# A spectral filter beside an expert router: the row transform split 64 by 32 instead of 128 by 16, in f32 on 64 by 64 pieces of the array

## The chip, the core and the metric

The kernel runs on one NeuronCore of a Trainium2 chip. The metric is device time in microseconds of one execution. The engines are named as in the profile: PE is TensorE's matmuls, PEld its weight loads, DVE VectorE, ACT ScalarE, POOL GpSimd, SP the engine whose queue issues the DMAs.

## What is computed

x is 2048 tokens by 576 numbers. After a layer norm two branches are added to x: A filters it in the two-dimensional Fourier domain, B is a router over 64 experts that picks, in each of 32 heads, the best of 8 keys twice.

```python
def _A_ref(x, w_r, w_i):
    X = rfft2(x, axes=(-2, -1))
    X = X * (w_r + 1j * w_i)
    return irfft2(X, (S, D), axes=(-2, -1))

def _B_ref(x, w_q, k1, k2, u, v):
    q = einsum("nd,dhc->nhc", xf, w_q)
    s1, s2 = q[..., :dk] @ k1.T, q[..., dk:] @ k2.T
    top_e = argmax(s1) * E + argmax(s2)
    act = gelu(einsum("nd,nhkd->nhk", xf, u[top_e]))
    return einsum("nhk,nhk,nhkd->nd", g, act, v[top_e])

xn = layernorm(x)
return x + _A_ref(xn, A_w_r, A_w_i) + _B_ref(xn, B_w_q, B_k1, B_k2, B_u, B_v)
```

With one expert for each head, g is 1. Since only the largest score matters, the kernel multiplies w_q by differences of keys (`fold_part`), and gets all scores of a token from x in one product (`scores`).

## The kernel before

The tokens are split 128 by 16: tile t holds the 128 tokens 16 n + t, so a transform over tokens is a transform of 128 points inside a tile and one of 16 points across tiles. In order of the data:

- `ln` takes the statistics of the tiles as they land (VectorE, for six tiles ACT). `folds(t)` folds the 576 columns twice, about 288 and about 144, into cosine and sine parts (names `t` and `A` in the profile), scales the 128-point matrix by the tile's deviation (`Rs`) and copies the 33 leftover columns three times (`yl`).
- `dft128(t)` multiplies in f32: four matmuls `Rs,A` and two `Rs,yl`. An f32 matmul leaves two records in the trace, one for each pass. The product is parted into f16 high and low halves in `AB` (ACT, then VectorE), the leftover columns in `ABL`, whose rows 0 to 32, 33 to 65 and 66 to 98 hold the low and twice the high half.
- `fold_part(b, s)` is the product with the keys, f32, four pieces of 32 columns side by side (`w,KP`), on data that arrive by 32 transfers of 576 KB through five buffers; `fold_scale`, `fold_end` and `fold_last` bring it to `MU` and `MUL` in f16 halves.
- `d_fwd(g)` does the column transform for one sixteenth of the frequencies, out of `AB` and `ABL` (needs all sixteen `dft128`); its result is again parted in f16 halves (`A`). `s_fwd(g)` does the 16-point transform of two groups, 48 f16 matmuls on four 64 by 64 pieces of the array. `s_mul(g)` multiplies by the filter: two products on VectorE (`t`), two sums on GpSimd (`y`), a parting into f16 halves (`yh`) on ACT and GpSimd, and the leftover columns (`yl`) on ACT.
- `s_inv(g)` transforms back, 36 f16 matmuls on two 64-row pieces; `AB` and `ABL` are written again.
- `scores(r)`, `route(r)` and `combine(r)` treat two tiles of tokens each: 28 matmuls of 512 columns, the maxima and masks on VectorE, and the gathered weights `CAT` (inside `MT`).
- `d_inv(t)` is the column transform back (evicted by ACT, VectorE and GpSimd), `fin(t)` the 128-point transform back (f32, `A,c`) with the experts' sum (`vS,MT`) in the same PSUM tile; VectorE adds x and SP writes out.

`allmax` gets scales for the f16 halves as largest values: a transpose on TensorE, a maximum on VectorE, a matmul that spreads it.

The order of all instructions is made while the program is built: `_Plan` records operations, and `forward` places them by a table of priorities (`RANK`), its own costs, and PSUM places with limits for each kind of tile. All are issued through one helper line, so every row of the profile has the line L527 and is told apart by its tiles.

Of the kernel before, what the change touches and what calls it, by code (L numbers as in the profile page):

```python
# [10 lines left out]
F32 = mybir.dt.float32  # L11
# [4 lines left out]
OP = mybir.AluOpType  # L16
AX = mybir.AxisListType.X
# [14 lines left out]

def _consts():
    pi2 = 2 * np.pi
    n1 = np.arange(128)
    R = np.zeros((128, 16, 4, 2))
    for k in range(64):
        g, a = divmod(k, 4)
        if k == 0:
            R[:, g, a, 0] = 1.0  # L40
            R[:, g, a, 1] = (-1.0) ** n1
        else:
            R[:, g, a, 0] = np.cos(pi2 * (k * n1 % 128) / 128)
            R[:, g, a, 1] = -np.sin(pi2 * (k * n1 % 128) / 128)
    R = _clean(R.reshape(128, 128))
    c32 = np.stack([R * 2.0 ** -7, R.T * 0.5, np.eye(128)], 1).astype(np.float32)

    U = np.zeros((16, 16, 4, 2, 16, 2, 4))
    V = np.zeros_like(U)
    n2 = np.arange(16)[:, None]  # L50
    k2 = np.arange(16)[None, :]
    kk = np.zeros((16, 16, 2, 4), int)
    for g in range(16):
        for a in range(4):
            k1 = 4 * g + a
            if k1 == 0:
                for s in range(2):
                    ph = pi2 * ((64 * s + 128 * k2) * n2 % 2048) / 2048
                    U[g, :, a, s, :, s, a] = np.cos(ph)
                    V[g, :, a, s, :, s, a] = -np.sin(ph)  # L60
                    kk[g, :, s, a] = 64 * s + 128 * np.arange(16)
            else:
                ph = pi2 * ((k1 + 128 * k2) * n2 % 2048) / 2048
                for s, sg in ((0, 1), (1, -1)):
                    U[g, :, a, 0, :, s, a] = np.cos(ph)
                    U[g, :, a, 1, :, s, a] = np.sin(ph)
                    V[g, :, a, 0, :, s, a] = -sg * np.sin(ph)
                    V[g, :, a, 1, :, s, a] = sg * np.cos(ph)
                    kk[g, :, s, a] = (sg * (k1 + 128 * np.arange(16))) % 2048
    U = _clean(U.reshape(16, 128, 128))  # L70
    V = _clean(V.reshape(16, 128, 128))
# [7 lines left out]
    def halves(m):  # L79
        return np.concatenate([m[:, :64, :64], m[:, 64:, 64:]], 1)  # L80
# [50 lines left out]
    return c32, c16, s16, kk, ll  # L131


INF = float("inf")

CHANGE = 97.0

# [159 lines left out]
class _Plan:  # L297
# [7 lines left out]
    def cost(self, eng, m, out, ins, kw):  # L305
        n = 1
# [927 lines left out]
```

## Time and profile before

| | |
|---|---|
| median of 3 runs | 222.79 us (221.79 to 223.17) |
| span of the profiled execution | 220.8 us (its own time is not given apart) |
| moved by DMA | 43.43 MB, 197 GB/s in the mean |
| largest loads | wq: 32 of 576 KB; xT: 16 of 320 KB; W: 8 of 578 KB; x: 3 of 1154 KB and 2 of 577 KB |

The page cuts the span into 40 slices of 5.5 us; each digit is the busy share of a slice in tenths, PEclk the clock granted to TensorE:

```profile
PE   0079789999999999899998999899999899999993
DVE  1886999998599879639999998999999999999973
ACT  2096987986499788986769658585652323332330
POOL 3987887960209962854598349687946656686890
PEclk9999999999999999999999999999999999999999
DMA  6999999999999991634246310410000012123225
```

TensorE begins at the third slice. The DMA engines are full in the first fifteen slices and have little to do after that. From the twentieth slice TensorE and VectorE are both near full, while ACT empties towards the end.

### The profile page before, as it was taken

How to read it: one execution, taken by the hardware profiler on the slowest of the kernel's cores; microseconds unless marked ns; L12 is line 12 of the kernel's file. 1: busy time of each engine (PE TensorE's matmuls, PEld its weight loads, DVE VectorE, ACT ScalarE, POOL GpSimd, SP SyncE). 2: the span in 40 equal slices, each digit the busy share in tenths (PEclk: the TensorE clock that was granted, in tenths of full speed). 3: DMA queues.
4: the chain of work that ended last, by engine and by line, in shares of the span. 5: the costliest groups of instructions: out<-in, count | busy, mean ns of one | idle time of the engine just before them, and what ended most of it. 6: DMA issues, size and time to landing. Idle time of an engine off the chain costs nothing.

```text
span 220.8 us, 5961 instructions
## 1 busy us (share of the span) xinstructions
PE 196.7 (89%) x2287; PEld 134.9 (61%) x2287; DVE 193.2 (88%) x423; ACT 136.8 (62%) x297; POOL 146.0 (66%) x201
## 2 busy tenths in 40 slices
PE   0079789999999999899998999899999899999993
PEld 0048367766866658466565666455566577788872
DVE  1886999998599879639999998999999999999973
ACT  2096987986499788986769658585652323332330
POOL 3987887960209962854598349687946656686890
PEclk9999999999999999999999999999999999999999
DMA  6999999999999991634246310410000012123225
GB/s 205 405 425 416 408 410 405 389 354 353 367 410 411 406 370 64 202 98 109 96 123 196 118 56 11 148 39 4 1 3 0 0 56 107 53 109 125 91 113 210
DMA packets 14572, 43.43 MB, mean 197 GB/s; under 512 B 1872, under 2 KB 4688, under 8 KB 14160
## 3 DMA queue, kind: packets, MB, share of 16 engines
q1 hardware_dynamic: 14544, 43.05, 52.5%
q8 instruction: 18, 0.29, 0.5%
q14 instruction: 10, 0.08, 0.1%
HBM read 38.33 MB, written 4.72 MB: 195 GB/s over the span
## 4 chain that ended last, share of the span: by engine, by line
PE 48%; DVE 23%; ACT 13%; issue 6%; DMA 5%; POOL 3%; SPq 0%; DVEq 0%; POOLq 0%; ACTq 0%
PE banks L527 48%; DVE t L527 5%; DMA xf<-in_xT_dram 4%; DVE w L527 4%; DVE MT L527 3%; DVE A L527 3%; ACT t L527 2%; ACT xf L527 2%; DVE mx L527 2%; DVE AB L527 2%; DMA kT<-in_kT_dram 2%; ACT AB L527 1%; POOL yh L527 1%; DVE st L527 1%; ACT A L527 1%
## 5 line engine op out<-in xcount | busy, mean ns | idle before, releaser
L527 PE MATMUL banks<-MU,xT 128*128 128x512 f16 x192 | 47.9, 379 | 1.0 <-ACT A L527 0.6
L527 POOL TENSOR_TENSOR xT<-xf,xT 128x640 f16<-128x640 f32 x16 | 23.2, 1455 | 19.5 <-ACT xf L527 19.5
L527 PE MATMUL banks<-c,AB 128*128 128x145 f16 (+1 forms) x384 | 34.6, 227 | 0.0
L527 PEld LDWEIGHTS <-xT 128*128 128x128 f16 x224 | 20.6, 99 | 21.9 <-issue 1.3
L527 PEld LDWEIGHTS <-AB 128*128 128x128 f16 x384 | 31.7, 122 | 3.4 <-issue 1.6
L527 POOL TENSOR_TENSOR A<-t 128x145 f32<-128x145 f32 (+2 forms) x48 | 30.3, 647 | 4.0 <-DVE t L527 1.5
L527 POOL TENSOR_TENSOR y<-t,t 128x289 f32<-128x289 f32 x32 | 21.6, 697 | 14.7 <-DVE t L527 14.5
L527 POOL TENSOR_TENSOR yh<-y,yh 128x578 f16<-128x578 f32 x16 | 23.4, 1470 | 6.8 <-issue 3.0
L527 POOL TENSOR_TENSOR t<-XN 128x289 f32<-128x289 f32 x32 | 24.9, 799 | 4.3 <-DVE A L527 3.0
L527 DVE SCALAR_TENSOR_TENSOR t<-banks,wx,Wt 128x578 f32<-128x578 f32 x32 | 24.3, 808 | 0.3 <-PE banks L527 0.3
L527 DVE TENSOR_TENSOR AB<-banks,AB 128x512 f16<-128x512 f32 x32 | 21.6, 679 | 1.9 <-ACT AB L527 1.1
L527 PE MATMUL banks<-w,KP 128*32 128x288 f32 x256 | 21.5, 432 | 1.8 <-DMA w<-in_wq_dram 1.5
L527 ACT ACTIVATE yh<-banks,sc 128x580 f32<-128x580 f32 x16 | 11.7, 744 | 17.6 <-PE banks L527 13.6
L527 PE MATMUL banks<-Rs,yl 128*99 128x128 f32 x64 | 10.9, 302 | 13.1 <-ACT Rs L527 13.1
L527 ACT ACTIVATE AB<-banks 128x512 f16<-128x512 f32 x32 | 18.8, 590 | 4.6 <-PE banks L527 4.5
L527 PE MATMUL banks<-A,c 128*128 128x288 f32 x64 | 21.4, 416 | 0.0
L527 PE MATMUL banks<-c,ABL 99*128 99x289 f16 (+1 forms) x64 | 18.5, 289 | 2.3 <-DVE AB L527 0.9
L527 PEld LDWEIGHTS banks<-Rs,A 128*128 128x128 f32 x128 | 16.3, 202 | 3.7 <-DVE A L527 1.8
L527 DVE TENSOR_TENSOR ABL<-banks,ABL 33x256 f16<-33x256 f32 x32 | 12.9, 407 | 6.4 <-ACT AB L527 5.3
L527 PEld LDWEIGHTS banks<-Rs,yl 128*99 128x99 f32 x64 | 8.3, 180 | 16.6 <-ACT Rs L527 15.7
L527 PE MATMUL banks<-Rs,A 128*128 128x128 f32 x128 | 18.2, 292 | 0.0
L527 DVE TENSOR_REDUCE MT<-w 128x128 bf16<-128x896 bf16 (+1 forms) x16 | 18.1, 1143 | 0.1
(124 smaller groups left out, 433.5 us busy)
## 6 DMA issues: line engine op xcount, KB each, us to landing
w<-in_wq_dram SPq DMA_DIRECT2D x32, 576.0 KB, 7.6
xf<-in_xT_dram SPq DMA_DIRECT2D x16, 320.0 KB, 4.6
Wt<-in_W_dram SPq DMA_DIRECT2D x8, 578.0 KB, 7.3
out_dram<-XN SPq DMA_DIRECT2D x14, 288.0 KB, 2.1
XN<-in_x_dram SPq DMA_DIRECT2D x3, 1154.0 KB, 12.4
s<-in_s_dram SPq DMA_DIRECT2D x16, 192.0 KB, 3.4
XN<-in_x_dram SPq DMA_DIRECT2D x2, 577.0 KB, 4.9
c<-in_c_dram SPq DMA_DIRECT2D x1, 868.5 KB, 8.6
```

What stands on the lines that cost most here:

```text
L527: fn(*[x.place() if isinstance(x, _Ps) else x for x in args], **{k: x.place() if isinstance(x, _Ps) else x for k, x in kw.items()})
```

## The change

The tokens are split 64 by 32. A tile now holds two sets of 64 tokens, one in each half of the partitions, and the host puts rows and columns of x, W, v and the result into the order that this needs (`_tokens`, `_columns`). What follows from it, and what else is done:

- `folds` folds once; the second fold is done by `dft128`, which adds two f32 matmuls into one PSUM place, on two 64-row pieces. VectorE makes one sum of 289 numbers; GpSimd makes one difference, and copies the leftover columns for 14 tiles; seven scalings move from ACT to VectorE. Two more tiles have their statistics on ACT.
- `d_fwd`, `s_fwd`, `s_mul` and `s_inv` keep f32: no f16 halves of `A` and `y` are made. `s_fwd` is 16 f32 matmuls and `s_inv` 16, both on four 64 by 64 pieces. The leftover columns of two groups are transformed by `s_left`, parted, and stacked in `ABL` by six transfers (42 in all); the last two groups have `s_last`, without transfers.
- The second product of the filter for groups 4 to 15 is a copy on ACT and a product on GpSimd.
- `scores` has 24 and 2 matmuls, and four on 64 by 64 pieces. The maximum over seven keys is three pairwise steps. Four `xT` halves are parted on VectorE.
- `d_inv` takes `ABL` last; the second half of the even-odd sum is on GpSimd for six tiles and on VectorE for ten. `fin` takes two tiles: 8 f32 matmuls on 64 by 64 pieces, 4 on 64-row pieces and 4 whole ones.
- Scales come from `root`, a sum of squares by one matmul and a root by arithmetic on the float's bits, in ten places; one `allmax` is left.
- Sixteen matmuls on a constant tile stand first on TensorE.
- The order and the PSUM places are now lists of numbers (`ORDER`, `BANK`), and each GpSimd instruction with inputs waits for the last VectorE instruction ahead of it in the list that is marked as using their shared port.

The core of the diff:

```diff
+                if o.port and o.eng == "gpsimd" and held is not None:
+                    tc.add_manual_dep(o.last.ins, held.last.ins.name, WAIT, reason="the shared port")
+            if o.port and o.eng == "vector":
+                held = o
...
+    wu = AB[:, 0, 0, 0:512]
+    V.memset(wu, 1.0)
+    pw_ = PS("m", (128, 512))
+    for k in range(16):
+        P.matmul(pw_, wu[:, 0:128], wu, start=True, stop=True)
...
+    def root(src, k, dst, e):
+        p = PS("m", (128, 64))
+        P.matmul(p[:, :k], on[:, 0:1].to_broadcast([128, 128]), src, start=True, stop=True)
...
+        V.tensor_scalar(dst.bitcast(I32), v, 0.5, float(0x1FBD1DF5 + (e << 23)), op0=OP.mult, op1=OP.add)
...
     def folds(t):
-        G.tensor_tensor(F[:, 1, 0:145], e[:, 1, 0:145], e[:, 1, 288:143:-1], op=OP.add)
-        V.scalar_tensor_tensor(F[:, 0, 0:145], e[:, 0, 0:145], rr[:, 2, t:t + 1], e[:, 0, 288:143:-1],
-                               op0=OP.add, op1=OP.add)
-        (V if t in DV else G).tensor_tensor(F[:, :, 145:289], e[:, :, 143::-1], e[:, :, 145:289], op=OP.subtract)
...
+        e = T([128, 2, L], F32, "e", 4, "A2")
+        G.tensor_tensor(e[:, 1], xn[:, 0:L], xn[:, L:], op=OP.subtract)
...
+            V.scalar_tensor_tensor(e[:, 0], xn[:, 0:L], rr[:, 2, t:t + 1], xn[:, L:], op0=OP.add, op1=OP.add)
+        Rs = T([128, 2, 64], F32, "Rs", 3)
+        if t in RV:
+            V.tensor_scalar(Rs, Rm, rr[:, 0, t:t + 1], None, op0=OP.mult)
+        else:
+            A.activation(Rs, Rm, AF.Copy, scale=rr[:, 0, t:t + 1])
+        fl = T([128, 2, 3, 33], F32, "fl", 4, "y")
+        if t in FG:
+            G.tensor_copy(fl, e[:, :, 0:33].unsqueeze(2).to_broadcast([128, 2, 3, 33]))
+        else:
+            A.activation(fl, e[:, :, 0:33].unsqueeze(2).to_broadcast([128, 2, 3, 33]), AF.Copy)
...
-        for c in range(4):
-            b, s = divmod(c, 2)
-            o = 161 if s else 0
-            P.matmul(p[:, 0, 128 * c:128 * c + 128], F[:, b, o:o + 128], Rs, start=True, stop=True)
...
+        sm = [Rs[r, 0:1].to_broadcast([64, 2, 64]) for r in hs]
         for b in range(2):
-            P.matmul(p[:99, 1, 128 * b:128 * b + 128], FL[:, b, :, :].rearrange("p a b -> p (a b)"), Rs, start=True, stop=True)
+            for h, r in enumerate(hs):
+                P.matmul(p[:, h, 128 * b:128 * b + 128], e[r, b, 34:289:2], sm[h], start=True, stop=False, tile_position=(64 * h, 0))
...
+            for h, r in enumerate(hs):
+                P.matmul(p[:, h, 128 * b:128 * b + 128], e[r, b, 33:288:2], Rs[r], start=False,
+                         stop=True, tile_position=(64 * h, 0))
+        for b in range(2):
+            for h, r in enumerate(hs):
+                P.matmul(p[:99, h, 256 + 64 * b:320 + 64 * b], fl[r, b], Rs[r, 0], start=True,
+                         stop=True, tile_position=(64 * h, 0))
...
-        allmax(wm[:, g // 2:(g + n) // 2], n // 2, wx[:, 0, g:g + n].rearrange("p (k e) -> p k e", e=2), 4096.0)
+        root(wm[:, g // 2:(g + n) // 2], n // 2, wx[:, 0, g:g + n].rearrange("p (k e) -> p k e", e=2), 13)
...
-        t = T([128, 2, 2, L], F16, "A2", 2)
-        A.activation(t[:, 0], p[:, :, :L], AF.Copy)
-        V.tensor_tensor(t[:, 1], p[:, :, :L], t[:, 0], op=OP.subtract)
+        t = T([128, 2, L], F32, "A2", 4)
+        A.activation(t, p[:, :, :L], AF.Copy)
...
-                for ha, hb in ((0, 0), (1, 0), (0, 1)):
...
-                            s = S16[g + q][:, :384].rearrange("p (h w) -> p h w", h=2)
-                            P.matmul(ps[q][o:o + 64, m, :L], s[r, ha, 64 * w:64 * w + 64], A2[g + q][r, hb, b, :],
-                                     start=(n == 0), stop=(n == 5), tile_position=(64 * e, o))
-                    n += 1
+                for e in range(2):
+                    r = slice(64 * e, 64 * e + 64)
+                    for q in range(2):
+                        o = 64 * (e ^ q)
+                        P.matmul(ps[q][o:o + 64, m, :L], S32[g + q][r, 64 * w:64 * w + 64], A2[g + q][r, b, :],
+                                 start=(b == 0), stop=(b == 1), tile_position=(64 * e, o))
...
+        if g in SG:
+            A.activation(t2, p[:, :, :L], AF.Copy, scale=sw)
+            G.tensor_tensor(t2, t2, wi, op=OP.mult)
+        else:
+            V.scalar_tensor_tensor(t2, p[:, :, :L], sw, wi, op0=OP.mult, op1=OP.mult)
...
-        yh = T([128, 2, 2, L], F16, "yh", 2)
-        A.activation(yh[:, 0], y, AF.Copy)
-        G.tensor_tensor(yh[:, 1], y, yh[:, 0], op=OP.subtract)
...
-        Y[g] = (yh, yl)
+        Y[g] = y
...
-        for c in range(3):
+        y, s = Y[g], S32[g][:, 192:]
+        for c in range(2):
             for ri in range(2):
+                for z in range(2):
                     for e in range(2):
+                        r, o = slice(64 * e, 64 * e + 64), 64 * (e ^ z)
+                        P.matmul(p[o:o + 64, e ^ g % 2, c, :], y[r, ri, 161 * c + o:161 * c + o + 64],
+                                 s[r, 64 * ri:64 * ri + 128], start=(ri == 0), stop=(ri == 1), tile_position=(64 * e, o))
...
+    def s_left(g):
+        p = PS("c")
+        for ri in range(2):
+            for q in range(2):
+                y, s = Y[g + q], S32[g + q][:, 192:]
+                for e in range(2):
+                    r, o = slice(64 * e, 64 * e + 64), 64 * (e ^ q)
+                    P.matmul(p[o:o + 64, q, :128], y[r, ri, 128:192], s[r, 64 * ri:64 * ri + 128], start=(ri == 0),
+                             stop=(ri == 1), tile_position=(64 * e, o))
...
+        for k, n in ((1, 0), (2, 0), (0, 1)):
+            for e in range(2):
+                to = ABL[33 * k:33 * k + 33].rearrange("p b (a e n) -> p (b a) e n", a=2, e=2)
+                Q.dma_start(to[:, :, e, 32 * g:32 * g + 64], h[64 * e:64 * e + 33, n])
...
-            P.matmul(p[:, b, :290], ABLt[:99, b, :, t], il[:99, b, :], start=True, stop=False)
...
+        plan.cut()
+        for b in range(2):
+            P.matmul(p[:, b, :290], ABLt[:99, b, :, t], il[:99, b, :], start=False, stop=True)
...
+    EG = (0, 3, 6, 8, 11, 14)
...
-    def fin(t, y):
-            hs = slice(288 * h, 288 * h + 288)
-            P.matmul(p[:, h, :288], RT, y[:, hs], start=True, stop=False)
-            for q in range(2):
-                P.matmul(p[:, h, :288], CAT[:, t, :], vS[:, q, hs], start=False, stop=(q == 1))
...
+    def fin(t, ys):
...
+            for z in range(2):
+                for i in range(2):
+                    o = 64 * (z ^ i)
+                    P.matmul(ps[i][o:o + 64, h, :L], RT[64 * z:64 * z + 64], ys[i][64 * z:64 * z + 64, h],
+                             start=True, stop=False, tile_position=(64 * z, o))
+        for h in range(2):
+            for i in range(2):
+                r = slice(64 * i, 64 * i + 64)
+                P.matmul(ps[i][:, h, :L], CAT[r, t + i, :], vS[r, 1, L * h:L * h + L], start=False, stop=False,
+                         tile_position=(64 * i, 0))
+        plan.pack = set()
+        for i in range(2):
+            for h in range(2):
+                P.matmul(ps[i][:, h, :L], CAT[:, t + i, :], vS[:, 0, L * h:L * h + L], start=False, stop=True)
```

Where the lists move work, three places. On TensorE at the start of the program before (`yl` and `A` are the leftover columns and the folded tile, `w` a part of wq; x2 and x4 count matmuls in a row):

```order
L527 MATMUL banks<-Rs_102,yl_104 99x128 x2
L527 MATMUL banks<-Rs_103,yl_105 99x128 x2
L527 MATMUL banks<-w_119,KP 32x288 x4
L527 MATMUL banks<-w_118,KP 32x288 x4
L527 MATMUL banks<-Rs_103,A_1_99 128x128 x4
L527 MATMUL banks<-Rs_102,A_0_98 128x128 x4
```

and now, from the last of the sixteen constant matmuls on (`U` holds the leftover columns):

```order
L321 MATMUL banks<-AB 128x512
L321 MATMUL banks<-Rs_101,A_0_97 128x128 x8
L321 MATMUL banks<-Rs_101,U 99x64 x4
L321 MATMUL banks<-Rs_101,A_3_100 128x128 x8
L321 MATMUL banks<-Rs_101,U 99x64 x4
L321 MATMUL banks<-Rs_103,A_2_99 128x128 x8
```

The first pieces of wq have moved behind seven tiles of `dft128`.

On TensorE in the last stage before, one tile's `d_inv` ends and `fin` follows (`c` beside `AB` is the column matrix, beside `A` the matrix of `fin`):

```order
L527 MATMUL banks<-c_72,AB 128x145
L527 MATMUL banks<-A_0_98,c_68 128x288
L527 LDWEIGHTS MT
L527 MATMUL banks<-vS,MT 128x288
L527 LDWEIGHTS MT
L527 MATMUL banks<-vS,MT 128x288
```

and now, where the first pair's `fin` follows the `d_inv` of tile 4:

```order
L321 MATMUL banks<-c_72,ABL 128x290
L321 MATMUL banks<-A_0_97,c_68 64x289
L321 MATMUL banks<-A_1_98,c_68 64x289
L321 MATMUL banks<-A_0_97,c_68 64x289
L321 MATMUL banks<-A_1_98,c_68 64x289
```

The pieces of the two tiles alternate, and `ABL` has moved behind `AB`.

On SP's queue now, behind the last transfer of wq (`lo` are the parted leftover columns, `xf` the loads of xT, `Wt` the filter):

```order
L321 DMA ABL<-lo_131 33x4x64 x2
L321 DMA xf_122<-in_xT_dram 128x640
L321 DMA ABL<-lo_130 33x4x64
L321 DMA mk<-in_mk_dram 128x99
L321 DMA Wt_109<-in_W_dram 128x1156
L321 DMA ABL<-lo_130 33x4x64
L321 DMA xf_123<-in_xT_dram 128x640
```

Loads of xT and of the filter now stand behind transfers that wait for ACT and VectorE.

More of the change, by code (lines that the diff above doesn't have):

```diff
@@ L252 @@
 class _Op:
[L253 to L273 removed]
+    __slots__ = ("tiles", "eng", "calls", "cols", "stage", "port", "last")
 def size_of(dt):
@@ L643, in g @@
             plan.stage += 1
+            plan.names[plan.stage] = (f.__name__, *(x for x in args if isinstance(x, int)))
             return f(*args)
@@ L1124, in _body @@
+    for t, n in ((0, 1), (1, 3), (4, 4), (8, 4), (12, 4)):
         ln(t, n)
@@ L1169, in _body @@
         s_inv(g)
+        if g > 13:
+            s_last(g)
+        elif g % 2:
+            s_left(g - 1)
         if g + 2 < 16:
```

715 lines of the change are left out of this document (275 added, 440 removed), and 128 rows, old and new, of tables (BANK, ORDER, RANK).

## The prediction

> **What bounds the kernel now.** I read the page's head and chain first, then the busy times by stage, then TensorE's timeline for the price of each piece of work, then VectorE's groups. Head and chain of the page:
>
> ```profile
> span 220.8 us, 5961 instructions
> PE 196.7 (89%) x2287; PEld 134.9 (61%) x2287; DVE 193.2 (88%) x423; ACT 136.8 (62%) x297; POOL 146.0 (66%) x201
> PE 48%; DVE 23%; ACT 13%; issue 6%; DMA 5%; POOL 3%; SPq 0%; DVEq 0%; POOLq 0%; ACTq 0%
> ```
>
> Two engines are nearly full, so a change must relieve both. The kernel has one sharp seam: `d_fwd` needs all sixteen `dft128`, and the first matmul behind the last of them (uv_prep's `Wt,on`) starts at 54.95. The windows view split there (columns: length, then busy time of each engine, granted clock, DMA share, GB/s):
>
> ```profile
> core 0: us, PE busy (x) PEld busy (x) DVE busy (x) ACT busy (x) POOL busy (x), PEclk, DMA share, GB/s
> 0.00:54.95 54.95, 39.86 (x350) 28.03 (x350) 45.28 (x138) 38.03 (x106) 38.78 (x73) 1.00 0.98 377
> 54.95:217.40 162.45, 156.86 (x1941) 106.92 (x1937) 147.44 (x285) 98.78 (x192) 107.19 (x128) 1.00 0.38 137
> ```
>
> Stage 1, up to the seam, belongs to VectorE (45.28 us, while PE also has to wait for it); stage 2 belongs to TensorE (156.86 of 162.45) with VectorE 9% behind. Then 3.4 us follow. I forecast the three lengths apart.
>
> TensorE's prices come from its timeline, as start to next start where nothing waited (columns: start, length, instruction, count; an f32 matmul leaves two records, one for each pass, and the pairs of rows are not all adjacent):
>
> ```profile
> 42.55 0.60 PE L527 MATMUL banks<-Rs,yl 128*99 128x128 f32 x4
> 42.99 1.06 PE L527 MATMUL banks<-Rs,A 128*128 128x128 f32 x8
> 43.88 0.60 PE L527 MATMUL banks<-Rs,yl 128*99 128x128 f32 x4
> ...
> 49.19 0.69 PE L527 MATMUL banks<-w,KP 128*32 128x288 f32 x8
> 49.81 1.16 PE L527 MATMUL banks<-Rs,A 128*128 128x128 f32 x8
> ...
> 53.85 1.18 PE L527 MATMUL banks<-w,KP 128*32 128x288 f32 x16
> 54.95 1.10 PE L527 MATMUL banks<-Wt,on 128*128 128x64 f32 x8
> ...
> 110.02 1.68 PE L527 MATMUL banks<-A,s 64*64 64x289 f16 x48
> 111.63 1.04 PE L527 MATMUL banks<-MU,xT 128*128 128x512 f16 x4
> ...
> 120.11 0.84 PE L527 MATMUL banks<-s,yh 64*128 64x128 f16 x24
> 120.79 0.50 PE L527 MATMUL banks<-s,yl 64*99 64x128 f16 x12
> 121.22 1.04 PE L527 MATMUL banks<-MU,xT 128*128 128x512 f16 x4
> ...
> 142.47 2.76 PE L527 MATMUL banks<-MU,xT 128*128 128x512 f16 x12
> 145.07 0.27 PE L527 MATMUL banks<-c,wm 128*1 128x128 f32 x1
> ...
> 199.32 0.65 PE L527 MATMUL banks<-A,c 128*128 128x288 f32 x2
> 199.81 0.41 PE L527 MATMUL banks<-vS,MT 128*128 128x288 f16 x2
> 200.05 0.65 PE L527 MATMUL banks<-A,c 128*128 128x288 f32 x2
> ...
> 216.89 0.29 PE L527 MATMUL banks<-vS,MT 128*128 128x288 f16 x1
> ```
>
> So: an f32 pass over 128 columns costs 0.89/8 = 0.111 us, over 288 columns 0.49/2 = 0.245 (199.32 to 199.81). Four f32 pieces side by side, 32 columns of the array each, take 0.49 for eight passes (1.10 for 16 less 0.62 for 8): 0.061 a pass, exactly a quarter of 0.245. A pair in `s_fwd` is 1.61 for 48 f16 pieces of 64 by 64; one `s_inv` 0.68 + 0.43 = 1.11; 512 f16 columns 2.60/12 = 0.217; an f16 288-column matmul 0.12; a half tile of `fin` 0.73.
>
> **The change, part by part.** The VectorE groups that it touches (columns behind the bar: busy us, mean ns of one), and one GpSimd group:
>
> ```profile
> L527 DVE TENSOR_TENSOR A<-t 128x288 f32<-128x288 f32 x16 | 8.1, 504 | 1.9 <-PE banks L527 1.4 <-POOL t L527 0.6
> L527 DVE SCALAR_TENSOR_TENSOR A<-t,rr 128x145 f32<-128x145 f32 x16 | 6.5, 414 | 0.0
> L527 DVE BATCH_NORM_STATS2 st<-XN 128x6 f32<-128x288 f32 x20 | 7.8, 444 | 3.7 <-DMA XN<-in_x_dram 3.7
> L527 DVE CAST wt<-mk 128x448 bf16<-128x448 f32 x1 | 1.0, 1003 | 0.0
> L527 DVE TENSOR_TENSOR A<-banks,A 128x578 f16<-128x578 f32 x16 | 11.9, 751 | 0.5 <-ACT A L527 0.4
> L527 DVE SCALAR_TENSOR_TENSOR t<-banks,wx,Wt 128x578 f32<-128x578 f32 x32 | 24.3, 808 | 0.3 <-PE banks L527 0.3
> L527 DVE SCALAR_TENSOR_TENSOR t<-banks,sc,yh 128x290 f32<-128x290 f32 x16 | 8.2, 512 | 0.7 <-ACT yh L527 0.6
> L527 POOL TENSOR_TENSOR yh<-y,yh 128x578 f16<-128x578 f32 x16 | 23.4, 1470 | 6.8 <-issue 3.0 <-ACT yh L527 2.2 <-POOL y L527 1.5
> ```
>
> Stage 1 goes by VectorE. From its 45.28 us fall 16 second folds (8.1), 16 short sums (6.5), four statistics (1.8; the mean is 0.444) and the cast that now stands behind the seam (1.0). In come 16 sums of 289 numbers, not shown before: 0.414 is the price of half the width, 0.512 that of 290 from PSUM; I take 0.5, nearest to the second, 8.0 in all. In come 7 scalings of 128 numbers: between 0 and 0.414, taken as 0.2, so 1.4. Left are 37.3. VectorE's first work came at 4.63, and idled 54.95 - 4.63 - 45.28 = 5.0 inside the stage:
>
> ```profile
> 4.63 1.54 DVE L527 BATCH_NORM_STATS2 st<-XN 128x6 f32<-128x288 f32 x4 [3.66 <-DMA XN<-in_x_dram]
> ...
> 10.80 0.85 DVE L527 SCALAR_TENSOR_TENSOR A<-t,rr 128x145 f32<-128x145 f32 x1
> ```
>
> The first load is one tile in place of two, so I start at 3.9 and keep 2 of the 5 idle: the seam lies at 3.9 + 37.3 + 2 = 43.2. Lowest: no idle, scalings free, sums at 0.414: 38.4. Highest: all 5 idle, scalings at 0.414, sums at 0.85 as in the last row, which has half the width: 53.3. ACT's 38.0 loses 14 copies and 7 scalings and gains the sums of two tiles and three squarings: even, and next in line behind VectorE. GpSimd's 38.8 falls by a second fold and an addition a tile. TensorE is no limit there: a tile of `dft128` was 0.44 + 0.89 = 1.33, and is now 16 passes two side by side (0.89) and 8 short ones, between 0.22 (64 columns at a quarter of 0.111) and 0.48 (0.119 a pass in the `Wt,on` row, half of it): at most 1.37. The 16 dummy matmuls stand ahead of all data; their cover is the wait for x.
>
> Stage 2 goes by TensorE, against 162.45:
> - fold matmuls: 52 stood behind the seam, now 80: 56 passes at 0.061, +3.4.
> - `s_fwd`: 48 f16 pieces become 16 f32 pieces, 32 passes of 289 columns, a quarter of 0.245 each: 1.96 for 1.51 without the shape switch, eight pairs: +3.6.
> - `s_inv`: 1.11 becomes 32 passes at a quarter of 0.111, 0.89; `s_left` adds 16 such passes in 7 pairs, `s_last` two times 16: 14.2 + 3.1 + 0.9 for 17.8, +0.4.
> - `scores`: two of 28 matmuls of 0.217 become four pieces side by side (0.22): -0.2 each of eight, -1.7.
> - `fin`: a pair of tiles was 4 x 0.73 = 2.93; now 16 passes at 0.061, four half-height pieces two by two (0.24) and four whole ones (0.49): 1.71. Eight pairs: -9.9.
> - ten guards lose one of two short matmuls, about 0.11 from start to start (145.07 stands for it): -1.1.
> - switches between piece shapes: 63 behind the seam in both orders, 0.
>
> Sum -5.3. VectorE there loses the 16 low halves (12.0) and twelve products (9.7), gains ten second halves in `d_inv` (5.1 at 0.512), so its 147.4 falls to about 131, 83% of the stage, and should not hold TensorE. The twelve products go to ACT (12 copies) and GpSimd (12 at 1.47, while 16 subtractions of the same size leave it). I keep the stage's other 5.6 us (162.45 - 156.86) as they are: 157.15. The 42 row transfers of `s_left` stand ahead of loads on SP's queue:
>
> ```profile
> L527 SPq DMA_DIRECT2D w<-in_wq_dram x32: 327/328/647, 3.5 to 72.7; - x32
> out_dram<-XN SPq DMA_DIRECT2D x4, 144.0 KB, 1.8
> ```
>
> At 0.33 us an issue they take 13.8 us of a queue that is nearly idle, and land in 1.8 us or more (the smallest transfer shown). The cover is `scores(7)` and four `s_inv` between the last of them and `d_inv(0)`, some 10 us; without it the first `d_inv` would stand 2 to 4 us. The new waits of GpSimd for VectorE cost GpSimd up to one VectorE instruction each; behind them stand the y sums that `s_inv` needs, and GpSimd's idle third covers it. What they save VectorE I leave out.
>
> The end was 220.8 - 217.4 = 3.4; three of four halves now pass VectorE after nearly the same matmul, one more of about half a microsecond: 4.0.
>
> **Sum.** 43.2 + 157.15 + 4.0 = 204.35 us of span, for 220.8. The median of the runs, 222.79, lies 1.99 over this span (no separate time of the profiled execution is given), so 206.3.
>
> **Rivals.** *Slower: the f32 pieces run two at a time.* In `s_fwd`, `fin` and `s_left` the two row halves write one PSUM bank at once. Were they to take turns, 256 + 128 passes would cost 0.061 more and 112 passes 0.028 more: +26.6, 233. It decides from 62% of that on. Against it: the row at 110.02 has the same arrangement in f16, 48 pieces in 1.61, 0.034 each, a quarter of 0.12; and the fold's f32 pieces, in other shapes, run at a quarter. The Trainium skill ("TensorEngine Tiling (Array Packing)", Gotcha 1: PSUM Pressure) says that different row tiles cannot access one PSUM bank simultaneously; by that rule this rival would hold and the sum would be 233, but the row at 110.02 disagrees at 0.034 a piece. I leave it 6%.
>
> *No change: collisions of VectorE and GpSimd.* This row of the w tiles (shortest, median and longest ns) shows one form at 410 and at 1639:
>
> ```profile
> L527 DVE TENSOR_TENSOR w<-MT,iv x8: 410/426/1639, 110.8 to 201.0; 128x512 bf16<-128x512 bf16 x8
> ```
>
> If each of the twelve new GpSimd products stretches one VectorE step so, and VectorE is then last, 12 x 1.23 = 14.8 come back: 221. For it: VectorE is 91% busy now; against it: 16 GpSimd passes of that size go, and the waits. 10%.
>
> *Faster still: no idle.* The seam at 38.4 and 4.8 of the 5.6 idle gone: 204.35 - 4.8 - 4.8 + 2 = 196.7. For it: VectorE's share falls by 8 points; against it: TensorE waits for chains too. 15%.
>
> **How the numbers follow.** My forecast has 69% (its own range 199 to 217, from the seam's ends less some idle at the low one). The range 196 to 217 takes in the third rival and the seam's upper end (216.4), and leaves out the first and most of the second. A measurement of this kernel tells about 1% from no change. Faster by over 1% (under 220.6): 0.69 + 0.15 + about half of the second rival, 0.89; within 1%: 0.05; slower: 0.06.
>
> **What would show it.** Right: the first `d_fwd` matmul near 44; `s_fwd` pairs at about 2.0 us, `s_inv` at 0.9, a pair of `fin` at 1.7 to 1.9; VectorE under 85% behind the seam. Wrong: passes of 64-wide pieces above 0.08 us over 289 columns (first rival); bf16 steps of VectorE of over 1 us beside GpSimd products (second); `d_inv` waiting for a row transfer; a seam past 50.

## The result, and the profile after

Measured side by side, five runs each: 223.17 us before (221.79 to 224.22), 206.7 us after (204.99 to 210.08). The ratio is 0.9255, with a 95% interval of 0.9199 to 0.9312: faster, by 16.5 us. The forecast was 206.3. The profiled execution of the changed kernel took 204.99 us, its span is 203.2.

The head of the page of the changed kernel, the line of the chain of waits by engine, and then its windows view, cut at the seam (first `Wt,on`, 41.66) and where the chain leaves TensorE for the last time (197.40, called the last matmul below):

```profile
span 203.2 us, 6358 instructions
PE 190.7 (94%) x2511; PEld 126.5 (62%) x2511; DVE 160.2 (79%) x383; ACT 124.0 (61%) x272; POOL 105.9 (52%) x166
PE 79%; DVE 10%; DMA 6%; issue 1%; ACT 1%; DVEq 0%; SPq 0%; ACTq 0%
```

```profile
core 0: us, PE busy (x) PEld busy (x) DVE busy (x) ACT busy (x) POOL busy (x), PEclk, DMA share, GB/s
0.00:41.66 41.66, 35.89 (x497) 26.97 (x497) 35.03 (x106) 34.32 (x93) 19.61 (x55) 1.00 0.94 361
41.66:197.40 155.74, 154.58 (x2019) 99.58 (x2015) 123.83 (x275) 89.32 (x180) 85.54 (x110) 1.00 0.53 180
197.40:203.20 5.80, 0.24 (x2) 0.00 (x0) 1.37 (x3) 0.40 (x1) 0.80 (x1) 0.81 0.53 194
```

Two things are to be seen. The chain, of which TensorE had 48%, is now 79% TensorE: one engine carries the kernel. And the second stage, where TensorE stood still for 5.6 of 162.45 us, has 155.74 - 154.58 = 1.2 us left of that. The five runs spread over 5 us and this profile is of the fastest: six kernels below that leave this stage as it is have 2.2 to 4.2 us idle there in their profiles, 0.7 to 3.1 of it in waits for loads of `w`. Against the forecast:

| | before | forecast | measured |
|---|---|---|---|
| seam | 54.95 | 43.2 | 41.66 |
| stage 2, TensorE's work | 156.9 | 151.55 | 154.6 |
| stage 2, TensorE idle | 5.6 | 5.6 | 1.2 |
| end, behind the last matmul | 3.4 | 4.0 | 5.8 |
| span | 220.8 | 204.35 | 203.2 |

TensorE's timeline after: one tile of `dft128` and the start of the next, one pair of `s_fwd`, one `s_inv`, one pair of `fin` (three rows) and what follows it:

```profile
35.28 1.17 PE L321 MATMUL banks<-Rs,A 64*128 64x128 f32 x16
36.29 0.48 PE L321 MATMUL banks<-Rs,U 64*99 64x64 f32 x8
36.61 2.37 PE L321 MATMUL banks<-Rs,A 64*128 64x128 f32 x32
...
46.68 2.18 PE L321 MATMUL banks<-A,s 64*64 64x289 f32 x32
48.80 0.30 PE L321 MATMUL banks<-c,ABL 99*128 99x289 f16 x1
...
78.38 1.14 PE L321 MATMUL banks<-s,U 64*64 64x128 f32 x32
79.44 1.66 PE L321 MATMUL banks<-w,KP 128*32 128x288 f32 x24
...
191.03 1.21 PE L321 MATMUL banks<-A,c 64*64 64x289 f32 x16
192.17 1.03 PE L321 MATMUL banks<-vS,MT 64*128 64x289 f16 x8
193.13 1.21 PE L321 MATMUL banks<-A,c 64*64 64x289 f32 x16
```

From start to start: a tile of `dft128` 1.33; a pair of `s_fwd` 2.12 for 32 passes, 0.066 each with the switch of shape, so four pieces do run side by side in f32; `s_inv` 1.06; a pair of `fin` 2.10. The groups of VectorE and GpSimd that the prediction priced:

```profile
L321 DVE SCALAR_TENSOR_TENSOR t<-banks,wx,Wt 128x578 f32<-128x578 f32 x20 | 15.7, 813 | 2.4 <-PE banks L321 2.1
L321 DVE SCALAR_TENSOR_TENSOR A<-XN,rr 128x289 f32<-128x289 f32 x16 | 8.1, 530 | 0.3 <-POOL rr L321 0.2
L321 DVE TENSOR_TENSOR w<-w,MT 128x512 bf16<-128x512 bf16 x16 | 6.2, 415 | 0.0
L321 DVE TENSOR_SCALAR Rs<-c,rr 128x128 f32<-128x128 f32 x7 | 2.5, 352 | 0.0
L321 POOL TENSOR_TENSOR t<-t,Wt 128x578 f32<-128x578 f32 x12 | 15.6, 1314 | 21.7 <-ACT t L321 16.4
```

### The profile page after: what moved, and what is told of

Its sections match the earlier page's. It is cut to its first block, busy times and chain, and to the rows that moved or that the text cites. A ratio compares the mean times of both kernels' runs of the same rounds, so it can differ in the third digit from the quotient of the medians.

```text
span 203.2 us, 6358 instructions
## 1 busy us (share of the span) xinstructions
PE 190.7 (94%) x2511; PEld 126.5 (62%) x2511; DVE 160.2 (79%) x383; ACT 124.0 (61%) x272; POOL 105.9 (52%) x166
## 4 chain that ended last, share of the span: by engine, by line
PE 79%; DVE 10%; DMA 6%; issue 1%; ACT 1%; DVEq 0%; SPq 0%; ACTq 0%
PE banks L321 79%; DMA Wt<-in_W_dram 4%; DMA XN<-in_x_dram 2%; DVE st L321 2%; DVE AB L321 2%; DVE A L321 1%; DVE w L321 1%; DVE rr L321 1%; DVE t L321 1%; DVE mx L321 1%; DVE XN L321 0%; DVE Rs L321 0%; DVE mv L321 0%; DVE ABL L321 0%; ACT AB L321 0%
## 5 line engine op out<-in xcount | busy, mean ns | idle before, releaser
L321 PEld LDWEIGHTS <-xT 128*128 128x128 f16 (+1 forms) x240 | 20.7, 99 | 27.4 <-issue 5.0
L321 POOL TENSOR_TENSOR U<-t,t 128x289 f32<-128x289 f32 x32 | 21.7, 703 | 22.0 <-DVE sc L321 15.7
L321 POOL TENSOR_TENSOR t<-t,Wt 128x578 f32<-128x578 f32 x12 | 15.6, 1314 | 21.7 <-ACT t L321 16.4
L321 POOL TENSOR_TENSOR xT<-xf,xT 128x640 f16<-128x640 f32 x12 | 16.8, 1403 | 15.4 <-ACT xf L321 5.5
L321 POOL TENSOR_TENSOR A<-t 128x289 f32<-128x289 f32 x32 | 21.3, 699 | 2.8 <-DVE MT L321 2.5
L321 PE MATMUL banks<-Rs,A 64*128 64x128 f32 x256 | 19.1, 288 | 3.3 <-ACT Rs L321 1.4
L321 ACT ACTIVATE AB<-banks 128x512 f16<-128x512 f32 x32 | 18.9, 596 | 3.9 <-PE banks L321 3.2
L321 PEld LDWEIGHTS banks<-Rs,A 64*128 64x128 f32 x256 | 16.7, 195 | 5.8 <-ACT Rs L321 3.4
L321 PE MATMUL banks<-s,U 64*64 64x128 f32 x624 | 20.3, 272 | 0.0
L321 PEld LDWEIGHTS banks<-s,U 64*64 64x64 f32 x624 | 17.8, 133 | 2.5 <-issue 1.1
L321 PE MATMUL banks<-A,s 64*64 64x289 f32 x256 | 18.6, 408 | 0.0
L321 ACT ACTIVATE xT<-xf,bx 128x640 f16<-128x640 f32 x16 | 13.1, 828 | 2.5 <-DMA xf<-in_xT_dram 2.3
## 6 DMA issues: line engine op xcount, KB each, us to landing
ABL<-lo SPq DMA_DIRECT2D x42, 16.5 KB
```

The costliest lines, as they stand in the source:

```text
L321: o.last = fn(*[x.place() if isinstance(x, _Ps) else x for x in args], **{k: x.place() if isinstance(x, _Ps) else x for k, x in kw.items()})
```

## Experiments

All are edits of the changed kernel (median 206.7, seam 41.66, last matmul ending at 197.40, ratio 0.9255 to the kernel before).

### What sets the seam

`vec_less`, less work for VectorE, in `dft128`:

```diff
         V.tensor_tensor(lo[:33], l[:33], lo[:33], op=OP.subtract)
+        plan.ops[-1].calls = []
```

> Leaves out the subtraction of the leftover rows' high half on VectorE in all 16 dft128 (so rows 0 to 32 of ABL hold the high half, and what is computed from them differs): 16 x 0.402 us = 6.4 us less of VectorE ahead of the seam, nothing else moved. Theory A (the prediction's: VectorE holds stage 1): the seam moves from 41.66 to 35 to 37, the time falls by 5 to 6 us, to about 201. Theory B (TensorE has held stage 1 since 17.5 us, as the chain of waits of the changed kernel has it): the seam stays within 1 us of 41.7 and the time within 1% of 206.7.

206.43 us, ratio 0.9226 (0.9162 to 0.929). The seam is the first row of `Wt,on`; in the changed kernel it comes so:

```profile
39.58 2.15 PE L321 MATMUL banks<-w,KP 128*32 128x288 f32 x32
41.66 1.33 PE L321 MATMUL banks<-Wt,on 128*128 128x64 f32 x10
```

and in this one so:

```profile
38.27 2.50 PE L321 MATMUL banks<-w,KP 128*32 128x288 f32 x32
40.70 1.33 PE L321 MATMUL banks<-Wt,on 128*128 128x64 f32 x10
```

VectorE lost 6.4 us, 4.6 of them ahead of the seam (30.42 busy there for 35.03), and the seam came 1.0 earlier: theory B. The fold matmuls ahead of the seam take 2.50 for 2.15 here: the chain of this kernel runs through a load of `w` that landed at 40.03, while they ran. So the loads stand close behind TensorE as the next to hold the seam.

`vec_more`, more work for VectorE, in `folds`:

```diff
             V.scalar_tensor_tensor(e[:, 0], xn[:, 0:L], rr[:, 2, t:t + 1], xn[:, L:], op0=OP.add, op1=OP.add)
+            plan.ops[-1].calls *= 2
```

> Issues each of the 16 sums of 289 numbers on VectorE (A<-XN,rr, 0.53 us) twice: 8.5 us more of VectorE ahead of the seam. Theory A (VectorE holds stage 1): seam at 50, time +8.5. Theory B in its strict form (TensorE holds it, VectorE has only the 1.2 us idle left between its first work at 5.46 and the seam): seam at 48 to 49, time +6 to +7.5. Theory B in its loose form (much of VectorE's 35.03 us ahead of the seam is work that the seam doesn't need): seam moves by under 4 us.

215.63 us, ratio 0.966 (0.9599 to 0.9721):

```profile
50.10 1.33 PE L321 MATMUL banks<-Wt,on 128*128 128x64 f32 x10
```

All of the 8.5 us arrived: the seam moved by 8.4, the time by 8.9. TensorE ran some of its early tiles slowly here (last section), which may be a part of it, but long behind them, before the tile at 40.80, it waited 2.92 us for VectorE's `rr`. So VectorE has no room ahead of the seam either, though taking work off it there brings little.

`te_more_1`, more work for TensorE, in `dft128`, behind the four short matmuls:

```diff
                 P.matmul(p[:99, h, 256 + 64 * b:320 + 64 * b], fl[r, b], Rs[r, 0], start=True,
                          stop=True, tile_position=(64 * h, 0))
+        plan.ops[-1].calls *= 2
```

> Issues the four short matmuls of each dft128 (the leftover rows, 8 passes, 0.32 us) twice: 5.1 us more of TensorE ahead of the seam, of which 12 tiles or 3.8 us lie behind 17.48. Theory A (VectorE holds stage 1, TensorE has 5.8 us idle there): the seam moves by under 1 us. Theory B (TensorE holds it from 17.5 on): the seam moves by 3.5 to 4.5 us, to 45.2 to 46.2, and the time by as much, to about 210.5.

209.74 us, ratio 0.9378 (0.9315 to 0.944):

```profile
44.56 1.33 PE L321 MATMUL banks<-Wt,on 128*128 128x64 f32 x10
```

The seam moved by 2.9 of the 3.8 us that lie behind 17.48, the time by 3.0; theory A allowed under 1. Taken together: from 17.5 us on TensorE's own string of work holds the seam, and the sums and scalings of VectorE, which feed it tile by tile, are level with it. Work added to either moves the end; work taken from VectorE alone brought about 1 us. Taking work from TensorE alone was not tried.

### What the dummy matmuls do

`no_dummies`, in the loop that issues everything (`self.few` are the first four TensorE operations, four dummy matmuls each):

```diff
+        self.few = [i for i, o in enumerate(self.ops) if o.eng == "tensor"][:4]
...
+            if i in self.few:
+                o.calls = o.calls[:1] if i == self.few[0] else []
             for fn, args, kw in o.calls:
```

> Issues one of the 16 dummy matmuls at the start in place of 16, 5.7 us less of TensorE ahead of the first data. Theory A (the prediction's: they stand under the wait for x and cost and bring nothing): seam within 0.5 us of 41.7, time within 1%. Theory B (they bring something: without them the first dft128 tiles run at a lower rate): the first tiles of dft128 take longer than the 1.33 us from start to start that they take now, and the seam moves back by 1 us or more; over 1% if the whole of the first 17 us suffers. Theory C (they are in the way): the first dft128 matmul comes before 7.84 and the seam comes earlier.

208.62 us, ratio 0.9289 (0.9199 to 0.9378), which overlaps that of the changed kernel: in the time it can't be told. The timeline of this kernel can tell it:

```profile
7.93 2.08 PE L324 MATMUL banks<-Rs,A 64*128 64x128 f32 x16 [5.84 <-ACT Rs L324]
...
11.15 2.08 PE L324 MATMUL banks<-Rs,A 64*128 64x128 f32 x16 [0.54 <-ACT Rs L324]
...
13.63 2.02 PE L324 MATMUL banks<-Rs,A 64*128 64x128 f32 x16
15.44 0.82 PE L324 MATMUL banks<-Rs,U 64*99 64x64 f32 x8
16.05 1.30 PE L324 MATMUL banks<-Rs,A 64*128 64x128 f32 x16
```

The same 16 records take 2.02 to 2.08 us in the first three tiles, and 1.30 from the fourth on; with the dummies the first took 1.22. The seam came at 42.98, 1.3 late: theory B. The Trainium skill ("TensorE: Matmul & The Clock Gate", "Part 1: The HAM clock gate") says that TensorE starts at half rate and reaches its full rate after about 4 us of sustained matmuls. The trace agrees in kind: 2.08 for 1.22 is 1.7 times as long; with the pauses between the tiles the change came about 8 us after the first of them.

### What holds stage 2

`te_more_2`, more work for TensorE, in `s_inv` behind its 16 matmuls:

```diff
+        if g % 2 == 0:
+            plan.ops[-1].calls *= 2
```

> Issues the 16 matmuls of s_inv (32 passes, 0.93 us) twice for the eight even g: 7.4 us more of TensorE behind the seam, all else as it is. Theory A (the prediction's: TensorE holds stage 2): the last matmul and the time move by 6.5 to 7.5 us, to about 213.9. Rival (VectorE, GpSimd or the loads hold part of it, and TensorE waits unseen): under 4 us.

213.89 us, ratio 0.9561 (0.9506 to 0.9617): +7.2 for 7.4 added. TensorE holds stage 2, nearly one to one: theory A. In the profile it stands idle for 1.6 us of the stage, so the added work went straight into the time.

`products_on_vec` put VectorE's second product at the place of GpSimd's. It read its PSUM bank after the next matmuls had taken it, so that part of the filter is not what the kernel computes, and its 216.84 us say nothing of the sharing.

> Undoes the sharing of the filter: the twelve second products go back to VectorE (0.81 us each, 9.7 us), and ACT's twelve copies (8.7 us) and GpSimd's twelve products (15.6 us) go. Theory A (the prediction's: TensorE holds stage 2 and VectorE, at 80%, has room): VectorE rises to some 86% behind the seam, and the time changes by less than 1% (204.7 to 208.8). Rival (the sharing is what took VectorE off the path): +5 to +10 us.

`products_on_vec2`, in `s_mul`, with VectorE's product where ACT's copy stood:

```diff
             A.activation(t2, p[:, :, :L], AF.Copy, scale=sw)
+            op = plan.ops[-1]
+            op.eng, op.port = "vector", False
+            op.calls = [(nc.vector.scalar_tensor_tensor, (t2, p[:, :, :L], sw, wi), dict(op0=OP.mult, op1=OP.mult))]
             G.tensor_tensor(t2, t2, wi, op=OP.mult)
+            plan.ops[-1].calls = []
```

> Undoes the sharing of the filter as the kernel before had it: for the twelve g in SG, VectorE makes the second product straight from PSUM, at the place in the order where ACT's copy stood (0.81 us each, 9.7 us more for VectorE; 8.7 us less for ACT, 15.6 us less for GpSimd). The run before this one put VectorE's product at the place of GpSimd's, later, so that it read its PSUM bank after the next matmuls had taken it, and its +10 us say nothing of the sharing. Theory A (the prediction's: TensorE holds stage 2, VectorE at 80% has room): +0 to +2 us on 206.7. Rival (VectorE's order is tight between the filter and the scores, and the sharing took it off the path): +5 to +10 us.

211.99 us, ratio 0.9476 (0.9435 to 0.9517): +5.3. Its windows view over stage 2 (from its seam to VectorE's first step behind its last matmul), and the first row of TensorE's waits (total us, times, longest):

```profile
41.32:203.84 162.52, 155.72 (x2019) 99.61 (x2015) 130.75 (x288) 81.09 (x168) 69.70 (x98) 1.00 0.51 172
```

```profile
PE banks L321 <- DVE t L321: 4.4, 6, 1.5
```

TensorE's work is the same within 1.2 us (155.72 for 154.58); its idle time is 6.8 for 1.2. VectorE is busy 130.75 of 162.52, 80%, the share that it has in the changed kernel too (123.83 of 155.74), and still TensorE waits for it six times, for `t`, the filter's products. In the kernels that leave this stage as it is, such waits come to 0.7 us at most. So theory A falls, and the share alone doesn't tell whether VectorE holds TensorE.

`no_port_wait`, in the same loop of issues:

```diff
-                if o.port and o.eng == "gpsimd" and held is not None:
-                    tc.add_manual_dep(o.last.ins, held.last.ins.name, WAIT, reason="the shared port")
```

> Takes out the added waits of GpSimd for the VectorE instruction ahead of it. Theory A (the waits are what ended the collisions: w<-w,MT at 415 ns now and 587 before): the bf16 steps of VectorE rise again, some to over 1 us; w<-w,MT back to 550 to 600, VectorE +4 to +8 us in all; with TensorE holding stage 2 the time rises by under 1% to 2%. Rival (GpSimd's own work and its place ended them): w<-w,MT stays under 450 and the time within 0.5%.

212.75 us (median of three runs; a fourth is told at the end), ratio 0.9498 (0.9418 to 0.9577): +6.1. The windows view over stage 2, and three rows of the `MT` tiles of VectorE (shortest, median and longest ns):

```profile
43.04:205.48 162.44, 155.16 (x2019) 99.30 (x2015) 130.55 (x274) 88.63 (x180) 86.74 (x110) 1.00 0.50 170
```

```profile
L321 DVE TENSOR_SCALAR MT<-MT x16: 163/170/1371, 106.3 to 195.4; 128x16 int32<-128x16 f32 x16
L321 DVE TENSOR_TENSOR MT<-w x8: 210/222/1420, 100.1 to 169.7; 128x128 bf16<-128x128 bf16 x8
L321 DVE TENSOR_TENSOR MT<-MT,fm x8: 274/284/1387, 108.8 to 195.6; 128x128 int32<-128x128 int32 x8
```

In the changed kernel the longest of these are:

```profile
L321 DVE TENSOR_SCALAR MT<-MT x16: 166/170/736, 103.9 to 187.5; 128x16 int32<-128x16 f32 x16
L321 DVE TENSOR_TENSOR MT<-w x8: 211/219/226, 97.7 to 162.5; 128x128 bf16<-128x128 bf16 x8
L321 DVE TENSOR_TENSOR MT<-MT,fm x8: 277/284/294, 105.2 to 187.7; 128x128 int32<-128x128 int32 x8
```

Without the waits single steps of VectorE grow from 0.2 to 0.3 us to 1.4, near the length of one large GpSimd instruction (`t<-t,Wt` 1314 ns, `xT<-xf,xT` 1403 in the mean; each of the six longest steps lies beside one of these), and VectorE's work in stage 2 rises from 123.83 to 130.55. The medians don't move: the collisions are few, and `w<-w,MT`, which I had expected at 550 to 600, hardly had any (430 in the mean), so for that group it was the rest of the change that ended them. They cost time all the same: TensorE again does the same work, 155.16, and idles 7.3 us, 4.9 of them in waits for VectorE (3.4 for `t`) and 2.2 for loads; 1.4 us more came ahead of the seam (43.04). Theory A, with another set of instructions hit, and with 3% in place of the 1 to 2% that I gave.

`no_rows`, in `s_left`:

```diff
                 Q.dma_start(to[:, :, e, 32 * g:32 * g + 64], h[64 * e:64 * e + 33, n])
+                plan.ops[-1].calls = []
```

> Leaves out the 42 row transfers of s_left (so rows of ABL keep what stage 1 left there). They issue in some 36 us of SP's queue now (0.85 us each), and not in the 0.33 that the prediction took. Theory A (hidden: nothing waits for the last of them, and the loads behind them on the queue are early): time within 0.5% of 206.7. Rival (loads of W, xT and s behind them on the queue come late because of them, or VectorE's 1.8 us of waits for them matter): faster by 1 to 3 us, with shorter TensorE waits between 70 and 110.

206.14 us (203.87 to 208.16, four runs), for 206.7 with them. Runs that spread so far can't tell 1 us, but the profiles agree: spans of 203.0 and 203.2, stage 2 of 156.07 and 155.74, and no shorter waits of TensorE from 70 to 110 us. The transfers are hidden, as forecast, at two and a half times the forecast price of an issue.

### What makes a piece of the array cheap

`by_quadrant`, the loops of `s_fwd`:

```diff
-        for m in range(2):
-            for b in range(2):
-                w = (0, 1, 1, 2)[2 * m + b]
-                for e in range(2):
-                    r = slice(64 * e, 64 * e + 64)
-                    for q in range(2):
-                        o = 64 * (e ^ q)
+        for e in range(2):
+            r = slice(64 * e, 64 * e + 64)
+            for q in range(2):
+                o = 64 * (e ^ q)
+                for m in range(2):
+                    for b in range(2):
+                        w = (0, 1, 1, 2)[2 * m + b]
```

> The same 16 f32 pieces of an s_fwd pair, written quarter by quarter: the four pieces of one 64 by 64 quarter of the array one after another, then those of the next. Theory A (the quarter price of 0.061 us a pass comes from neighbours in the order that lie in four different quarters): a pair takes far longer than the 2.12 us of now; with each pass alone at the 0.245 us of a full-array pass 32 x 0.245 = 7.8 us, +5.7 a pair, +46 in eight pairs, some 250 us. Theory B (it comes from the small size alone, in whatever order): 2.1 us and the time unchanged. In between (two quarters overlap where they meet): +15 to +30 us.

227.89 us (two runs), ratio 1.0185 (1.0151 to 1.0219): 1.8% above the kernel before. One pair of `s_fwd` and the row behind it:

```profile
46.56 5.26 PE L321 MATMUL banks<-A,s 64*64 64x289 f32 x32
51.75 0.30 PE L321 MATMUL banks<-c,ABL 99*128 99x289 f16 x1
```

5.19 us for 2.12, with the same 16 matmuls. They are not wholly one after another (that would be 7.8), but the nest of four loops is worth 21 us. Single rows show how. In the changed kernel four passes start within 0.02 us, and the next four 0.24 to 0.29 us later. Here the eight passes of the first quarter start as far apart, one by one, from 46.56 to 48.32, the price of a pass over the whole array; the second quarter's first pass starts at 47.59, beside the fifth of the first. So a small piece is cheap only beside pieces of other quarters, and with this order two quarters at most run side by side. The Trainium skill ("TensorE: Matmul & The Clock Gate", "Part 3: Packing small matmuls") has matmuls start and end in program order, without reordering. The rows agree in part: the quarters come in their order, but three passes of the first quarter start behind the second quarter's first, at 47.83, 48.07 and 48.32.

### A version with earlier loads, and one with two queues at the end

`loads_early`, behind the table of the order:

```diff
+EARLY = (398, 284, 397, 282, 281)
+_rest = [i for i in ORDER if i not in EARLY]
+_at = _rest.index(303)
+ORDER = (*_rest[:_at], *EARLY, *_rest[_at:])
```

> Moves five loads (v, u, two of the filter W and c16, 2.5 MB) on SP's queue ahead of the load of w that waits from 11.7 to 22.6 us for a buffer, where the queue now stands still and the transfers fall to 216 GB/s. Theory A (the loads hold TensorE back up to the first score at 87.69, as the chain's DMA W piece from 62.2 to 69.5 has it): W lands some 2 us earlier, the waits of TensorE at 67.6 to 71 shrink, the first score comes 1 to 2.5 us earlier and the time falls as much. Theory B (TensorE, busy 45.34 of those 46.03 us, holds it): the first score moves by under 0.7 us, the time by less than can be told. Theory C (the loads of x that are still in transit at 11 to 15 us, or the next w, suffer): seam later by 1 us or more.

211.95 us, ratio 0.9483 (0.9456 to 0.951): 5.2 slower, where I had hoped for 1 to 2.5 less. TensorE's timeline of this kernel:

```profile
32.88 1.18 PE L326 MATMUL banks<-w,KP 128*32 128x288 f32 x16 [2.37 <-DMA w<-in_wq_dram]
34.24 1.19 PE L326 MATMUL banks<-w,KP 128*32 128x288 f32 x8 [0.19 <-DMA w<-in_wq_dram]
35.36 2.08 PE L326 MATMUL banks<-Rs,A 64*128 64x128 f32 x16
```

Theory C. The hole in the transfers was filled (416 GB/s from 20 to 25 us, for 216), but the next `w` came late, and the fold matmuls stand in line ahead of `dft128`: 2.4 us of waiting. Behind that wait TensorE is slow again, 2.08 for a tile that takes 1.2, so a wait of 2.4 costs 3.7 at the seam (45.39).

`loads_early_tail` is the same with one edit in `fin`:

```diff
                 Q.dma_start(os[:, t + i, L * a:z], x[:, L * a:z])
+                if t > 13 and i:
+                    plan.ops[-1].calls = [(nc.scalar.dma_start, *plan.ops[-1].calls[0][1:])]
```

> As loads_early, and the last tile's two halves go out on ACT's queue, beside SP's. Theory A (the end of 5.8 us from the last matmul is longer than predicted because SP issues the last four transfers one after another, 0.58 us each, until 1.6 us after VectorE's last instruction): the end falls to 4.6 to 5.0 us, 0.8 to 1.2 us less in all than loads_early. Theory B (the end is the transfer itself and what follows it): 5.6 to 5.8 us, no change.

209.74 us, ratio 0.9379 (0.9342 to 0.9415), below `loads_early` by 2.2 us. The last rows of the queues, of the changed kernel first, then of this one:

```profile
198.06 2.31 SPq L321 DMA_DIRECT2D out_dram<-XN  x4
```

```profile
203.15 0.33 SPq L326 DMA_DIRECT2D out_dram<-XN  x1
```

```profile
202.84 0.89 ACTq L326 DMA_DIRECT2D out_dram<-XN  x2
```

With one queue the last transfer is issued at 200.37, 2.9 us after VectorE began its last instructions (197.43); with two at 203.73, 1.9 after (201.87). The end is 5.2 us for 5.8 in the changed kernel and 6.6 in `loads_early`. The twelve profiles with one queue have ends from 5.4 to 6.6, so one profile of 5.2 makes a gain of half a microsecond to one likely, not certain; of the 2.2 us, 1.2 lie ahead of the first score, which the edit doesn't touch. The queues split without the moved loads were not run, and neither version beats the changed kernel.

## Why the prediction was right, point by point

The total came out 1.2 us under the forecast span, in part by luck: the seam came 1.5 us early, stage 2 was 1.4 us shorter and the end 1.8 longer than forecast. Inside stage 2 TensorE's work was set 3 us too low and its idle time 4.4 too high.

**The first work, right.** Statistics began at 3.68, forecast 3.9.

**VectorE's prices in stage 1.** The sums took 0.53 each (taken as 0.5), the scalings 0.352 (0.2, at the upper side of the bounds 0 to 0.414). 35.03 us were busy for 37.3: one tile's evictions and some maxima moved behind the seam as well. VectorE's idle time there was about 3.5 us, for the 2 that the forecast kept.

**"Stage 1 goes by VectorE ... TensorE is no limit there": half right.** The relief of VectorE did bring the stage down to 41.7, but there TensorE stands level with it. The chain has TensorE nearly without a break from 17.48; 2.9 us of added matmuls went through, and 6.4 us less of VectorE brought 1.0. The number came out because the two limits lie within about 1 us of each other, which the working didn't show: it priced a tile of TensorE rightly (at most 1.37; 1.33 measured) and didn't add the tiles up.

**"The 16 dummy matmuls stand ahead of all data; their cover is the wait for x": right on the cost, wrong by what they bring.** They cost nothing (the first `Rs,A` starts at 7.84 with them, at 7.93 without) and save 1.3 us at the seam.

**Stage 2's sum, right in its kind, 3 us too hopeful.** The time from each row's start to the next row's start, less waits, summed by operands over stage 2 of each profile (half a microsecond more than the busy time above):

| part | before | after | change | forecast |
|---|---|---|---|---|
| fold matmuls | 7.8 | 11.2 | +3.4 | +3.4 |
| `s_fwd` | 13.5 | 17.9 | +4.4 | +3.6 |
| `s_inv`, leftover rows | 18.9 | 20.1 | +1.2 | +0.4 |
| scores | 50.5 | 47.9 | -2.6 | -1.7 |
| `fin` | 24.7 | 16.4 | -8.3 | -9.9 |
| guards | 3.1 | 1.9 | -1.2 | -1.1 |
| `d_fwd`, `d_inv` | 33.8 | 34.7 | +0.9 | 0 |
| rest | 5.2 | 5.0 | -0.2 | 0 |
| sum | 157.5 | 155.1 | -2.5 | -5.3 |

The largest miss is `fin`: 2.10 us a pair for 1.71, eight times (of which its higher cost before, 24.7 for the 23.4 of the working's prices, gives 1.3 back; by these prices the 9.9 is 9.8). Its f32 passes cost about what was forecast, 16 in 1.14 with a change of shape for 0.98 without, but the pair now changes the shape of its pieces three times and had none before. In single rows of the pair at 191.03 a change costs 0.10 us: half-height and whole matmuls start 0.13 apart among themselves, and 0.23 us pass from the last half-height one (192.30) to the first whole one (192.53). That is 0.3 of the 0.39. "switches between piece shapes: 63 behind the seam in both orders, 0" counted them over the stage, while the prices of `s_fwd` (without its switch) and `fin` were taken without any. By the rows' shapes the stage has as many changes after as before (73 in either trace), so they explain where the miss lies and not its sum; what makes up the rest is open.

**"I keep the stage's other 5.6 us": wrong, and this hid the miss.** The idle time fell to 1.2 (to 2.2 to 4.2 in the profiles of the other kernels with this stage). Two parts of the change keep it there, and the forecast gave neither a gain in idle time: the waits of GpSimd for VectorE ("What they save VectorE I leave out"; without them 7.3 us of idle, +6.1 in time) and the twelve shared products (without them 6.8 us, +5.3). In both, TensorE's waits for VectorE come to 4.8 or 4.9 us, where the other kernels have 1.0 at most. The two are not to be added, since either alone brings back about all of the old idle time. That VectorE, at 83% of the stage, "should not hold TensorE" came true for the changed kernel, but its reason, the share, doesn't carry it: with the products back on VectorE the share is the same 80%, and it did hold TensorE.

**VectorE's work in stage 2, 7 us too high.** It fell to 123.8, for the forecast 131. The low halves, the products and the second halves came as priced. Left out were the stretched steps: those more than 0.25 us over the median of their group exceed it by some 9.5 us in all before, by 1.4 after, and by 9.2 without the waits, so the waits are worth about 8 us to VectorE. Left out too were the leftover rows that `s_inv` no longer gives VectorE (`ABL<-banks,ABL`, 6.5 to 1.2), and, the other way, the four `xT` halves (3.9) and the halves of `s_left` (2.9).

**The end, mis-sized.** 5.8 for 4.0. The forecast added one more pass of VectorE; in the profile VectorE ends 1.4 us after the last matmul, and SP issues the last four transfers until 1.6 us after that.

**Covers.** The row transfers were hidden as said, though an issue took 0.83 us in the median, not 0.33 (three in 2.78 us from 76.41 on).

**Rivals.** "The f32 pieces run two at a time" is refuted by the rows: 0.066 a pass in `s_fwd` with both row halves in one bank. What four quarters at a time are worth `by_quadrant` shows: 21 us by order alone, in `s_fwd` alone. "Collisions" named a real mechanism; without the added waits it costs 6.1 us. Of "Faster still: no idle" stage 2's part nearly came true, and was given back in TensorE's work and at the end.

## What to carry to other kernels

A mean share of 80% doesn't clear an engine: ask whether its instructions come in time at the places where the full engine needs them, and take one off to see if the full engine's idle time changes while its work stays. Forecast work and idle time of the bounding engine apart, since errors of opposite sign in them can give a right total for a wrong reason. When small matmuls share the array, their order is part of the price, and each change of shape should be priced in the part where it happens.

## What the runs showed of the hardware

- TensorE's slow start can return after a pause. In `vec_more` a wait of 2.12 us was followed by three tiles at 2.08, 2.05 and 1.86 us, and the granted clock of the windows view is 0.66 from 10 to 20 us; in `loads_early` a wait of 2.37 had one such tile behind it. Not every pause does it: in `vec_more` the tile behind the wait of 2.92 us at 40.80 took 1.23, with a granted clock of 1.00. What decides between them is not shown. In `no_dummies` the clock column shows 1.00 from the start, while the records take 2.08 until 16 us; the first clock record of that trace stands at 16.3, so the length of a record tells the rate there, the column not.

```profile
12.32 2.08 PE L321 MATMUL banks<-Rs,A 64*128 64x128 f32 x16 [2.12 <-DVE A L321]
...
14.77 2.05 PE L321 MATMUL banks<-Rs,A 64*128 64x128 f32 x16
...
17.19 1.86 PE L321 MATMUL banks<-Rs,A 64*128 64x128 f32 x16
```

- One of the four executions of `no_port_wait` took 649.59 us, the others 210.58 to 213.48. What happened in it is open; no profile of it was taken.
